# Block-sparse attention and a SoLU layer in one kernel: centring tile u in place of w_out, with a new operation order

## The chip, the core and the metric

The kernel runs on one core of a Trainium2 chip. The metric is the device time of one execution in microseconds (us); lower is better. The core has five engines with queues of their own: TensorE (PE in the profile; PEld is its weight load), VectorE (DVE), ScalarE (ACT), GpSimd (POOL) and SyncE (SP), which here issues nearly all DMAs.

## The reference

q, k and v have shape (4, 8, 768, 64): four batches, eight heads, 768 positions in 24 blocks of 32. The attention is masked by blocks; its output is put through a feed-forward layer with a softmax gate and a layer norm.

```python
scores = scale * np.matmul(q, k.transpose(0, 1, 3, 2))
mask = np.abs(blk_i - blk_j) <= 1
mask = mask | (blk_i == 0) | (blk_j == 0) | (blk_i == n_blocks - 1) | (blk_j == n_blocks - 1)
...  # three sampled blocks for each row of blocks are added to the mask
attn = softmax(np.where(mask, scores, -1e9));  x = attn @ v      # x: 3072 x 512
h = x @ w_in                                                     # 3072 x 1024
solu = h * softmax(h)
ln = (solu - mean(solu)) / np.sqrt(var(solu) + 1e-06) * g_ln
out = ln @ w_out                                                 # 3072 x 512
```

## The kernel before, in words

All matmuls are in bf16. The mask is part of the score: keys and queries have 64 columns of data and 24 more (KR = 88), a selector of the own block on the key's side and a row of penalties on the query's side, so that a forbidden pair gets a large negative score.

**Attention.** For each batch `b`, each third of the queries `t` (256 positions) and each pair of heads `pr`, `attend` issues three groups of four score matmuls into `sbank` (L561), three exponentials of 128 x 1024 on ACT (L568), one group of 24 matmuls with v (`pv`, L581) into an `mbank`, a reciprocal (L590) and a normalization into tile `x` (L593). That is 144 score groups, 144 exponentials and 48 pv groups.

**Feed-forward.** For each third, x is transposed by a DMA (L623) or, in the first and last third, by PE (L613). `feed` then treats two tiles of 128 positions. For a tile: two groups of four matmuls of 512 columns into `hbank` (L643), an exponential with its sum (silu_e, L666), the product u (L669), its statistics (L676, L679), then on POOL `z2` (L682), `vr` (L685) and the power -1/2 `rs` (L718). Tile u is transposed by a DMA from SP's queue (`cross_u`, L749; the first tile by PE, L741), two groups of four matmuls (`out4`, L759) multiply it by `w_out_sb`, the result is scaled by `rs` (L767 on ACT, L769 on DVE) and stored (L773). The last two tiles have parts of their own, in halves (L643 into `tbank`, L692, L696, L702, L729, L782). There are 24 tiles. A tile u is held until its transpose has been read; there are three.

**Centring of w_out.** The mean that the layer norm takes off is taken off the weights instead. `wg` (L439) scales each of the eight 128-row chunks of w_out by g into scratch, `cs` (L448) sums them over all rows with eight matmuls by a matrix of ones, `wb` (L451) divides by 1024, and `wo` (L453) scales each chunk again and subtracts that mean row. All `out4` need `wo`.

**Opening.** For batch 0, keys and queries are cast (L295, L293), transposed by PE (L477) and copied to `kT[0]` and `qT[0]`. The selector is made on POOL (L307, L310), transposed by PE (`selp_tp`, L324) and copied by ACT (`selp`). The penalty rows come from small DVE operations up to `bar_b` (L346), and from `mask2` (L350) and `mcol` (L359) on PE. For later batches, `crossed` casts a pair of heads (cast6), transposes it by a DMA (L533) and splits it into the two heads' rows (`split`); these copies run by list on DVE, POOL or ACT, all at line L295 or L293. w_in is staged in `kT[1]` and `qT[1]`, and the mask rows of these two are copied from `kT[0]` and `qT[0]` by two DMAs (`m1dma`, L811 and L812).

**Order.** The kernel makes a list of 1159 operations and emits them in an order that is written out by hand (`ORDER`); `ENGINES` says which of them run on another engine than the one in the code, and `SPARES` lists dummy matmuls (L823) that are put in the order. Each engine takes its operations in that order and waits at the head of its queue, SP included: a DMA that has to wait holds up all DMAs behind it.

Of the kernel before, what the change touches and what calls it, by code (L numbers as in the profile page):

```python
# [871 lines left out]
```

## Time and profile before

| | us |
|---|---|
| median of three runs (208.11 to 209.76) | 208.84 |
| the profiled execution | 210.25 |
| its span in the trace | 208.5 |
| PE busy / ACT busy / DVE busy / POOL busy | 200.3 / 179.4 / 138.8 / 84.2 |
| DMA moved | 43.19 MB, 207 GB/s mean |

A row of the groups reads: line, engine, operation, output<-input, shapes, count | busy us, mean ns of one | idle time of the engine just before them, and what ended it. A row of the timeline or of the chain reads: start us, length us, what. A row of one tile's view reads: line, engine, operation, count: duration ns min/median/max, first and last start. "SPq" is SP's queue.

### The profile page before, as it was taken

The page shows a single profiled execution, that of the slowest core. Times are in us where ns is not written, and L with a number is a line of the kernel's source. Part 1 is how long each engine was busy: PE and PEld are TensorE (multiplying, and loading weights), DVE is VectorE, ACT ScalarE, POOL GpSimd, SP SyncE. Part 2 cuts the span into 40 slices and gives each one's busy share as a digit, 9 for nine tenths or more (in the row PEclk, how much of TensorE's full clock was granted, in tenths as well). Part 3 has the DMA queues.
Part 4 walks back from the last instruction along what each step waited for, and adds up shares of the span by engine and source line. Part 5 has one row for each costly group of instructions (what it writes and reads, how often), then busy time and mean ns, then how long its engine had stood idle before and what let it go on. Part 6 is the DMA issues. An engine that isn't in the chain of part 4 may idle for free.

```text
span 208.5 us, 5748 instructions
## 1 busy us (share of the span) xinstructions
PE 200.3 (96%) x2282; PEld 142.0 (68%) x2313; DVE 138.8 (67%) x306; ACT 179.4 (86%) x230; POOL 84.2 (40%) x158
## 2 busy tenths in 40 slices
PE   8999999999999999999799999999999999999993
PEld 4798876756667768566566767666767758666452
DVE  5586689999887555757676864754755565485840
ACT  3599999998999999999599998989989898876683
POOL 4235398185540647316640731683320211001271
PEclk9999999999999999999999999999999999999999
DMA  5999995999999998999899989995393314672534
GB/s 142 336 358 347 384 361 123 205 226 287 211 222 327 311 189 208 254 263 286 230 299 228 233 185 251 207 257 126 101 127 99 63 19 104 151 105 53 122 134 152
DMA packets 71736, 43.19 MB, mean 207 GB/s; under 512 B 53348, under 2 KB 67180, under 8 KB 71660
## 3 DMA queue, kind: packets, MB, share of 16 engines
q1 hardware_dynamic: 71672, 42.81, 84.9%
q8 instruction: 18, 0.29, 0.6%
q14 instruction: 10, 0.08, 0.1%
q10 hardware_dynamic: 36, 0.00, 0.0%
HBM read 23.07 MB, written 6.29 MB: 141 GB/s over the span
## 4 chain that ended last, share of the span: by engine, by line
PE 73%; DVE 12%; DMA 7%; ACT 3%; issue 2%; SPq 1%; ACTq 0%
PE sbank L561 22%; PE mbank L759 15%; PE hbank L643 14%; PE mbank L581 13%; DMA qx<-qb 4%; DVE w_out_sb L453 3%; PE abank L477 3%; ACT ex L568 2%; DMA xT<-x 2%; DVE u L669 2%; PE tbank L643 2%; PE sbank L823 2%; DVE x L593 1%; DMA out_dram<-ot 1%; DVE w_in_sb L295 1%
## 5 line engine op out<-in xcount | busy, mean ns | idle before, releaser
L568 ACT ACTIVATE ex<-sbank 128x1024 bf16<-128x1024 f32 x144 | 141.0, 1025 | 15.7 <-PE sbank L561 14.2
L561 PE MATMUL sbank<-qT,kT 88*128 88x256 bf16 x576 | 81.5, 272 | 0.5 <-DVE qT L295 0.3
L561 PEld LDWEIGHTS <-kT 88*128 88x128 bf16 x576 | 52.7, 97 | 19.2 <-issue 0.9
L759 PE MATMUL mbank<-w_out_sb,uT 128*128 128x512 bf16 x175 | 45.0, 379 | 0.8 <-DVE w_out_sb L453 0.3
L581 PEld LDWEIGHTS <-ex 128*128 128x128 bf16 x1152 | 40.8, 97 | 7.0 <-issue 1.3
L581 PE MATMUL mbank<-va,ex 128*128 128x65 bf16 x1152 | 42.3, 193 | 1.4 <-DVE x L593 1.3
L643 PE MATMUL hbank<-w_in_sb,xT 128*128 128x512 bf16 x157 | 41.9, 378 | 1.4 <-DMA xT<-x 0.3
L669 DVE TENSOR_TENSOR u<-hbank,e 128x1024 bf16<-128x1024 f32 x22 | 26.8, 1216 | 19.6 <-ACT e L666 15.7
L676 DVE BATCH_NORM_STATS2 bs<-u 128x6 f32<-128x512 bf16 x44 | 29.2, 679 | 0.2
L643 PEld LDWEIGHTS <-xT 128*128 128x128 bf16 x192 | 18.2, 97 | 15.0 <-DMA xT<-x 0.8
L759 PEld LDWEIGHTS <-uT 128*128 128x128 bf16 x184 | 17.6, 97 | 14.6 <-issue 0.8
L590 DVE RECIPROCAL r<-mbank 128x4 f32<-128x4 f32 x48 | 8.3, 175 | 25.7 <-PE mbank L581 25.5
L666 ACT ACTIVATE e<-hbank 128x1024 bf16<-128x1024 f32 x22 | 22.5, 1024 | 1.3 <-PE hbank L643 1.3
L685 POOL TENSOR_SCALAR vr<-z,mv 128x1 f32<-128x1 f32 x22 | 5.8, 266 | 39.0 <-DVE mv L679 38.0
L593 DVE TENSOR_TENSOR x<-mbank,r 128x256 bf16<-128x256 f32 x48 | 19.7, 415 | 0.8
L718 POOL TENSOR_TENSOR rs<-vr,neg_half 128x1 f32<-128x1 f32 x24 | 13.8, 579 | 0.8
L295 POOL COPY qT<-kc 64x768 bf16<-64x768 bf16 x10 | 8.9, 889 | 11.7 <-DMA kc<-qb 6.1
L769 DVE TENSOR_SCALAR ot<-mbank,rs 128x512 f32<-128x512 f32 x13 | 9.7, 745 | 5.7 <-PE mbank L759 3.1
L682 POOL TENSOR_TENSOR z<-z 128x1 f32<-128x1 f32 x22 | 4.7, 212 | 20.1 <-ACT e L666 19.7
L295 POOL CAST kb<-kst 128x768 bf16<-128x768 f32 x7 | 6.2, 892 | 15.3 <-DMA kst<-in_k_dram 8.8
L295 POOL COPY kT<-kc 64x768 bf16<-64x768 bf16 x13 | 11.0, 844 | 2.6 <-DMA kc<-kb 2.2
L295 POOL CAST va<-vst 128x768 bf16<-128x768 f32 x8 | 6.6, 827 | 7.4 <-DMA vst<-in_v_dram 7.3
(110 smaller groups left out, 165.5 us busy)
## 6 DMA issues: line engine op xcount, KB each, us to landing
vst<-in_v_dram SPq DMA_DIRECT2D x16, 384.0 KB, 5.0
out_dram<-ot SPq DMA_DIRECT2D x23, 256.0 KB, 2.4
kst<-in_k_dram SPq DMA_DIRECT2D x15, 384.0 KB, 4.7
qst<-in_q_dram SPq DMA_DIRECT2D x12, 384.0 KB, 5.3
w_out_f<-in_moe_w_out_dram SPq DMA_DIRECT2D x2, 1024.0 KB, 8.4
qst<-in_q_dram SPq DMA_DIRECT2D x4, 256.0 KB, 5.9
...
```

The source lines that it names most:

```text
L295: (nc.vector if o.eng == "DVE" else nc.gpsimd).tensor_copy(out=dst, in_=src)
L561: nc.tensor.matmul(s[:, m, :], kT[i][0:KR, pr, jc, hh, :], qT[i][0:KR, pr, 2 * t : 2 * t + 2, hh, :], start=(m % 2 == 0), stop=(m % 2 == 1))
L568: exs.append(op("exp", "ACT", lambda o, so=so: nc.scalar.activation(out=exb[o.slot], in_=sbank[so.slot], func=ACT.Exp, scale=scale), [so], ...
L581: nc.tensor.matmul(acc(o)[:, qt, hh, :], exb[exs[n].slot][:, m, qt * P : (qt + 1) * P], va[i][:, 2 * pr + hh, jc, :], start=first, stop=(n ...
L593: nrm = op("norm", "DVE", lambda o: nc.vector.tensor_tensor(out=xb[x_of[b, t].slot][:, :, 2 * pr * D : (2 * pr + 2) * D].rearrange("p a (h ...
L643: nc.tensor.matmul(d, xTb[xt[0].slot][:, qt, c, :], w_in_sb[n][:, c, :], start=(c == 0), stop=(c == KD - 1))
L666: zs = op("silu_e", "ACT", lambda o: nc.scalar.activation(out=eb[o.slots["e"]], in_=hb(), func=ACT.Exp, accum_out=zb[o.slots["z"]][:, 0:1] ...
L669: us = op("mult", "DVE", lambda o: nc.vector.tensor_mul(out=ub[o.slot], in0=hb(), in1=eb[zs.slots["e"]]), [zs], take="u", last_of=[(hs[0], ...
L676: bs.append(op("stats", "DVE", lambda o, n=n: nc.vector.bn_stats(out=bsb[(bs[0] if bs else o).slot][:, n, :], in_=ub[us.slot][:, w(o, n)]) ...
L718: rs = op("rs", "POOL", lambda o: nc.gpsimd.tensor_tensor(out=rsb[o.slot], in0=vrb[vr.slot], in1=neg_half, op=ALU.pow), [vr, c2], take="rs ...
L759: nc.tensor.matmul(mbank[m0.slot], uTb[ut[0].slot][:, KF // 2 * n + f, :], w_out_sb[n][:, f, :], start=(n == 0 and f == 0), stop=(n == 1 a ...
L769: nc.vector.tensor_scalar(out=otb[o.slot], in0=mbank[os_[0].slot], scalar1=rsb[rs.slot], scalar2=None, op0=ALU.mult)
```

## The change

- **Centring.** `wg` scales each chunk of w_out once, straight into `w_out_sb`, and for 22 of the 24 tiles that is the weight. For these tiles the product becomes `multa`, with an accumulator that gives the mean, and a new pass `cent` takes the mean off u in place (ten on DVE, twelve on POOL), ahead of the transpose and of the statistics. The last two tiles keep uncentred u and take centred weights, made late: three sums over the chunks (`ws4`, `ws2`, `ws1`, on POOL), one matmul `cs`, and the eight `wo` on DVE, into the space of `kT[0]` and `qT[0]` once batch 2 has been read.
- **Selector.** `selp_tp` and the ACT copy go; four selects on POOL (two for the first two columns of blocks, two for the other four) make the transposed selector directly. `mask2` needs only the first part.
- **Mask rows.** The two mask DMAs (`m1dmb`) read only the first pair's rows and broadcast them, and each waits for four of the eight w_in casts. The splits of batch 1 wait for those w_in casts whose staging space they overwrite.
- **Order.** ORDER, ENGINES and SPARES are new (1187 operations; 36 dummy matmuls, most of them of 128 columns). 12 `z2` and 9 `vr` are on DVE, all eight `wo` on DVE, five of eight `wg` and four of eight w_in casts on POOL, five of 23 scales on ACT (ten before), of the k, q and v casts 11 on DVE (18 before). Two query loads are issued ahead of the first key load.

```diff
-    st = op("selp_tp", "PE", selp_tp, [own, mids], take="m")
-    sels = op("selp", "ACT", lambda o: copy(
-        o, selp.rearrange("a c p -> a (c p)"), mbank[st.slot].bitcast(BF16)[0:NB, 0 : NCH * P]), [st], last_of=[st])
+    sels = []
+    for c0, c1 in ((0, 2), (2, NCH)):
+        a = op(f"selp{c1 - c0}", "POOL", lambda o, c0=c0, c1=c1: nc.gpsimd.affine_select(
+            out=selp[:, c0:c1], in_=nc.const_aps.tensor(1.0, (NB, c1 - c0, P), BF16), compare_op=ALU.is_ge,
+            fill=0.0, base=c0, channel_multiplier=-BLK, pattern=[[1, c1 - c0], [NCH, P]]))
+        sels.append(op(f"selp{c1 - c0}", "POOL", lambda o, c0=c0, c1=c1: nc.gpsimd.affine_select(
...
-    def w_out_g(c):
-        return exb[wg[c - c % 2].slot].rearrange("p (a m) t -> p a (m t)", a=2)[:, c % 2, :]
     def weigh(o, c):
-        d, s, k = w_out_g(c), w_out_f[c // 4][:, c % 4, :], g_sb[:, c : c + 1]
+        d, s, k = w_out_sb[c // 4][:, c % 4, :], w_out_f[c // 4][:, c % 4, :], g_sb[:, c : c + 1]
...
-        for c in range(KF):
-            nc.tensor.matmul(mbank[o.slot], onesf, w_out_g(c), start=(c == 0), stop=(c == KF - 1))
...
+    def centred_weights(free):
...
+        s4 = op("ws4", e, lambda o: add(o, level[1], w_out_sb[0].rearrange("p c d -> p (c d)"),
+                                        w_out_sb[1].rearrange("p c d -> p (c d)")), wg + free)
+        s2 = op("ws2", e, lambda o: add(o, level[2], level[1][:, 0 : 2 * d], level[1][:, 2 * d :]), [s4])
+        tot = level[1].bitcast(BF16)[:, 0:d]
+        s1 = op("ws1", e, lambda o: add(o, tot, level[2][:, 0:d], level[2][:, d:]), [s2])
+        cs = op("cs", "PE", lambda o: nc.tensor.matmul(mbank[o.slot], onesf, tot, start=True, stop=True), [s1, c1],
+                take="m")
...
-            us = op("mult", "DVE", lambda o: nc.vector.tensor_mul(
-                out=ub[o.slot], in0=hb(), in1=eb[zs.slots["e"]]), [zs],
+            um = op("multa", "DVE", lambda o: nc.vector.scalar_tensor_tensor(
+                out=ub[o.slot], in0=hb(), scalar=1.0 / d_ff, in1=eb[zs.slots["e"]], op0=ALU.mult, op1=ALU.mult,
+                accum_out=zb[zs.slots["z"]][:, 1:2]), [zs],
                 take="u", last_of=[(hs[0], hp), (zs, ("e",))])
+            us = op("cent", "DVE", lambda o: (nc.vector if o.eng == "DVE" else nc.gpsimd).tensor_scalar(
+                out=ub[um.slot], in0=ub[um.slot], scalar1=float(d_ff), scalar2=zb[zs.slots["z"]][:, 1:2],
+                op0=ALU.mult, op1=ALU.subtract), [um], last_of=[um, (zs, ("z",))])
...
-            mask1["k"] = op("m1dma", "SP", lambda o: nc.sync.dma_start(out=kT[1][MC], in_=kT[0][MC]), kdone + w_in_b)
-            mask1["q"] = op("m1dma", "SP", lambda o: nc.sync.dma_start(out=qT[1][MC], in_=qT[0][MC]), qdone + mq0 + w_in_b)
+            for nm, a, dep in (("k", kT, kdone[:2]), ("q", qT, [ready_q[0, 1, 0][0]] + mq0)):
+                mask1[nm] = op("m1dmb", "SP", lambda o, a=a: nc.sync.dma_start(
+                    out=a[1][MC], in_=a[0][MC, 0:1].broadcast_to([NB, NPR, NCH, 2, P])),
+                    dep + [w_in_n[n][c + (0 if nm == "k" else 2)] for c in range(2) for n in range(2)])
```

More of the change, by code (lines that the diff above doesn't have):

```diff
@@ L319 @@
     kheld = [own1] + kown[1:]
-    def selp_tp(o):
-        d = mbank[o.slot].bitcast(BF16)
-        for c in range(NCH):
-            nc.tensor.matmul(d[0:NB, c * P : (c + 1) * P], kc[0][:, c, 0, MC], ident, is_transpose=True,
-                             start=(c == 0), stop=(c == NCH - 1))
-    st = op("selp_tp", "PE", selp_tp, [own, mids], take="m")
-    sels = op("selp", "ACT", lambda o: copy(
-        o, selp.rearrange("a c p -> a (c p)"), mbank[st.slot].bitcast(BF16)[0:NB, 0 : NCH * P]), [st], last_of=[st])
+    sels = []
[4 more added lines that the diff above has]
+        sels.append(op(f"selp{c1 - c0}", "POOL", lambda o, c0=c0, c1=c1: nc.gpsimd.affine_select(
+            out=selp[:, c0:c1], in_=selp[:, c0:c1], compare_op=ALU.is_ge, fill=0.0, base=BLK - 1 - c0,
+            channel_multiplier=BLK, pattern=[[-1, c1 - c0], [-NCH, P]]), [a]))
     d2 = op("small", "DVE", lambda o: nc.vector.tensor_tensor(out=dist, in0=iota_d, in1=iota_d, op=ALU.mult),
@@ L340 @@
     static = op("small", "DVE", lambda o: nc.vector.memset(bar[1][:, 0 : NB : NB - 1], 0.0), [b1])
-    iof = op("small", "DVE", lambda o: nc.vector.tensor_copy(out=iota_f, in_=iota_k), [ik])
-    slo = op("small", "DVE", lambda o: nc.vector.tensor_copy(out=samp_f, in_=samp_i[:, :, 0]), [samp_dma])
+    iof = op("conv", "DVE", lambda o: copy(o, iota_f, iota_k), [ik])
+    slo = op("conv", "DVE", lambda o: copy(o, samp_f, samp_i[:, :, 0]), [samp_dma])
     prev, dep = bar[1], [static, iof, slo]
@@ L417, with staged @@
         for n in range(2)]
-    w_in_b = w_in_n[0] + w_in_n[1]
+    def staged(nm, pr):
+        c0 = 0 if nm == "k" else 2
+        return [w_in_n[n][c0 + c] for c in ((0,), (0, 1), (1,), ())[pr] for n in range(2)]
     g_load = op("g", "SP", lambda o: nc.sync.dma_start(out=g8, in_=moe_g_ln.rearrange("(c p) -> c p", p=P)))
@@ L440, in weigh @@
                                                                        op0=ALU.mult)
-    for c in range(KF):
-        wg.append(op("wg", "DVE", lambda o, c=c: weigh(o, c), [w_out_load[c // 4], g_cp],
-                     take=None if c % 2 else "ex", after=wg[c - 1 :] if c % 2 else ()))
-    def cs_mm(o):
-        for c in range(KF):
-            nc.tensor.matmul(mbank[o.slot], onesf, w_out_g(c), start=(c == 0), stop=(c == KF - 1))
-    cs = op("cs", "PE", cs_mm, wg + [c1], take="m", last_of=wg[::2])
@@ L451 @@
-    wb = op("wbar", "ACT", lambda o: nc.scalar.mul(out=wbar, in_=mbank[cs.slot], mul=1.0 / d_ff), [cs],
-            last_of=[cs])
-    wo = [op("wo", "DVE", lambda o, c=c: (nc.vector if o.eng == "DVE" else nc.gpsimd).scalar_tensor_tensor(
-        out=w_out_sb[c // 4][:, c % 4, :], in0=w_out_f[c // 4][:, c % 4, :], scalar=g_sb[:, c : c + 1],
-        in1=wbar, op0=ALU.mult, op1=ALU.subtract), [wb]) for c in range(KF)]
+    wg = [op("wg", "DVE", lambda o, c=c: weigh(o, c), [w_out_load[c // 4], g_cp]) for c in range(KF)]
@@ new lines, with add @@
+    w_end = kT[0].rearrange("p a b c d -> p (a b c d)")[:, 0 : KF * d_model].rearrange("p (f d) -> p f d", f=KF)
+    w_sum = qT[0].rearrange("p a b c d -> p (a b c d)").bitcast(FP32)
+    def centred_weights(free):
+        e, d = "DVE", d_model
+        level = [None, w_sum[:, 0 : 4 * d], w_sum[:, 4 * d : 6 * d]]
+        def add(o, dst, a, b):
+            (nc.vector if o.eng == "DVE" else nc.gpsimd).tensor_tensor(out=dst, in0=a, in1=b, op=ALU.add)
+        s4 = op("ws4", e, lambda o: add(o, level[1], w_out_sb[0].rearrange("p c d -> p (c d)"),
[5 more added lines that the diff above has]
+                take="m")
+        wb = op("wbar", "ACT", lambda o: nc.scalar.mul(out=wbar, in_=mbank[cs.slot], mul=1.0 / d_ff), [cs],
+                last_of=[cs])
+        return [op("wo", "DVE", lambda o, c=c: nc.vector.scalar_tensor_tensor(
+            out=w_end[:, c, :], in0=w_out_f[c // 4][:, c % 4, :], scalar=g_sb[:, c : c + 1], in1=wbar,
+            op0=ALU.mult, op1=ALU.subtract), [wb]) for c in range(KF)]
@@ L458 @@
+    w_last = []
     last_use = {}
@@ L465, in cast_v @@
         i = b % 2
-        ready_v[(b, pr)] = op("cast6", "POOL", lambda o: copy(
+        ready_v[(b, pr)] = op("cast6" if b == 0 else "castb", "POOL", lambda o: copy(
             o, va[i][:, 2 * pr : 2 * pr + 2, :, 0:D], vst[ld.slot]),
@@ L470, with turned @@
     a_ops = []
-    def turned(pr, src, held, s0, c0, c1, dst, deps, eng, release=(), rows=KR):
+    def turned(pr, src, held, s0, c0, c1, dst, deps, eng, release=(), rows=KR, after=()):
         n = c1 - c0
@@ L478, in tp @@
                                  ident, is_transpose=True, start=(k == 0), stop=(k == 2 * n - 1))
-        t = op(f"turn{2 * n}", "PE", tp, deps + [mids], take="a", last_of=release)
+        t = op(f"turn{2 * n}", "PE", tp, deps + [mids], take="a", last_of=release, after=after)
         a_ops.append(op(f"evac{2 * n}", eng, lambda o: copy(
@@ L499, in opening @@
             gq = turned(pr, qa, cq, 0, 0, 2, qT[0], [cq], "DVE", [cq], rows=D)
-            ga = turned(pr, kc, ck, 0, 0, 2, kT[0], [ck] + kown, "ACT", [ck])
+            ga = turned(pr, kc, ck, 0, 0, 2, kT[0], [ck, kown[0]], "ACT", [ck], after=kown)
             gb = turned(pr, kc, ck, 2, 2, 6, kT[0], [cr], "DVE", [ck] + kheld)
@@ L508, in opening @@
             gq = turned(pr, qa, cq, 0, 0, 2, qT[0], [cq] + qown, "DVE", [cq])
-            ga = turned(pr, kc, ck, 0, 0, 4, kT[0], [ck] + kown, "DVE", [ck] + kheld)
+            ga = turned(pr, kc, ck, 0, 0, 4, kT[0], [ck, kown[pr % NKC]], "DVE", [ck] + kheld, after=kown)
             gb = turned(pr, kc, ck, 4, 4, 6, kT[0], [ck], "DVE", [ck] + kheld)
@@ L530, in crossed @@
         st, cb, cx, dst = (kst, kb, kx, kT) if nm == "k" else (qst, qb, qx, qT)
-        ca = op("cast6", "POOL", lambda o: copy(
+        ca = op("castb", "POOL", lambda o: copy(
             o, cb[o.slot], st[ld.slot].rearrange("p h c d -> p c h d")), [ld], take=nm + "b", last_of=[ld])
@@ L536, in crossed @@
         for hh in range(2):
-            got.append(op("split", "DVE", lambda o, hh=hh: copy(
+            got.append(op("split", "POOL", lambda o, hh=hh: copy(
                 o, dst[i][0:D, pr, :, hh, :], cx[t.slot][hh * D : hh * D + D]),
-                [t, last_use.get((b - 2, pr))] + (w_in_b if b == 1 else []), last_of=[t]))
-        got += ([mask1["k"]] if nm == "k" else [mask1["q"]]) if b == 1 else []
+                [t, last_use.get((b - 2, pr))] + (staged(nm, pr) if b == 1 else []), last_of=[t]))
+        got += [mask1[nm]] if b == 1 else []
         if nm == "k":
@@ L676, in feed @@
                 bs.append(op("stats", "DVE", lambda o, n=n: nc.vector.bn_stats(
[L677 to L678 removed]
+                    out=bsb[(bs[0] if bs else o).slot][:, n, :], in_=ub[um.slot][:, w(o, n)]),
+                    [us] + bs, take=None if n else "bs", last_of=[um]))
             mv = op("aggr", "DVE", lambda o: nc.vector.bn_aggr(
@@ L748, in feed, with w2 @@
         else:
-            ut = [op("cross_u", "SP", lambda o: nc.sync.dma_start_transpose(out=uTb[o.slot], in_=ub[u0.slot]), [u0],
+            ut = [op("cross_u", "SP", lambda o: nc.sync.dma_start_transpose(out=uTb[o.slot], in_=ub[u0.slot]), [us],
                      take="uT", last_of=[u0])] * 2
         HD = d_model // 2
+        if last and not w_last:
+            w_last.extend(centred_weights([last_use[B - 2, pr] for pr in range(NPR)]))
+        wn = w_last if last else wg
+        def w2(f):
+            return w_end[:, f, :] if last else w_out_sb[f // 4][:, f % 4, :]
         if j < NF - 1:
@@ L782, in outp @@
                         nc.tensor.matmul(mbank[o.slot][:, 0:HD], uTb[ut[0].slot][:, f, :],
-                                         w_out_sb[f // 4][:, f % 4, cols], start=(f == 0), stop=(f == KF - 1))
-                oo = op("outh", "PE", outp, ut + wo, take="m", last_of=[ut[0]])
+                                         w2(f)[:, cols], start=(f == 0), stop=(f == KF - 1))
+                oo = op("outh", "PE", outp, ut + wn, take="m", last_of=[ut[0]])
                 def scaled(o, cols=cols, oo=oo):
```

38 lines of the change are left out of this document (19 added, 19 removed), and 118 rows, old and new, of tables (ENGINES, ORDER, SPARES).

## The prediction

> **What bounds the kernel now.** I read the page first (busy time, chain that ended last), then the chain in order of time, then busy time by stage, then the tiles that the change touches.
>
> ```profile
> PE 200.3 (96%) x2282; PEld 142.0 (68%) x2313; DVE 138.8 (67%) x306; ACT 179.4 (86%) x230; POOL 84.2 (40%) x158
> PE 73%; DVE 12%; DMA 7%; ACT 3%; issue 2%; SPq 1%; ACTq 0%
> ```
>
> A busy PE need not be a full one, so I count its work. The chain in order of time has the price of each group of matmuls when nothing is in its way (start, length, what); the group rows of the weight loads have the counts.
>
> ```profile
> 8.20 0.44 PE sbank L561 x4
> ...
> 12.30 0.45 PE abank L477 x8
> ...
> 20.55 0.73 PE mbank L581 x24
> ...
> 55.19 0.86 PE mbank L759 x4
> ...
> 64.52 0.86 PE hbank L643 x4
> ...
> 203.49 1.87 PE mbank L782 x16
> ```
> ```profile
> L561 PEld LDWEIGHTS <-kT 88*128 88x128 bf16 x576 | 52.7, 97 | 19.2 <-issue 0.9 <-DVE qT L295 0.4 <-POOL kT L295 0.4
> L581 PEld LDWEIGHTS <-ex 128*128 128x128 bf16 x1152 | 40.8, 97 | 7.0 <-issue 1.3 <-DVE x L593 0.5 <-ACT ex L568 0.4
> L643 PEld LDWEIGHTS <-xT 128*128 128x128 bf16 x192 | 18.2, 97 | 15.0 <-DMA xT<-x 0.8 <-issue 0.6
> L759 PEld LDWEIGHTS <-uT 128*128 128x128 bf16 x184 | 17.6, 97 | 14.6 <-issue 0.8
> ```
>
> Scores 144 x 0.44 = 63.4 us, pv 48 x 0.73 = 35.0, feeds 48 x 0.86 = 41.3, outputs 46 x 0.86 + 1.87 = 41.4; the transposes (8 in 0.45) come to about 8, the column sum of w_out to 8 matmuls of 0.215 = 1.7. That is 190.6 of useful PE work in a span of 208.5. The first score is at 8.2 and the last matmul ends at 205.4; about 0.9 of the work lies ahead of 8.2, so only some 7.5 us in between are lost. Busy time by stage shows where:
>
> ```profile
> 30.00:50.00 20.00, 19.23 (x202) 13.16 (x205) 19.87 (x35) 18.82 (x26) 12.55 (x16) 1.00 0.94 213
> 50.00:100.00 50.00, 49.55 (x570) 35.01 (x577) 34.47 (x72) 46.94 (x56) 23.01 (x40) 1.00 1.12 247
> 100.00:110.00 10.00, 8.47 (x96) 5.89 (x94) 6.80 (x15) 7.68 (x10) 4.78 (x9) 1.00 1.14 284
> 110.00:190.00 80.00, 78.77 (x927) 55.70 (x940) 49.42 (x108) 71.24 (x88) 23.42 (x48) 1.00 0.71 148
> ```
>
> Columns: stage, length, then PE, PEld, DVE, ACT, POOL busy with instruction counts, clock, DMA. From 50 to 100 and from 110 on PE is full at clock 1.00: nothing on another engine is worth time there, and any new wait costs its full length. Gains can come from PE work left out, from the start, from 30 to 50 (DVE busy 19.87 of 20) and from 100 to 110.
>
> **The change, part by part.** *w_out.* Before, w_out is scaled into scratch (L439), summed over its rows by 8 matmuls (L448) and scaled again with the mean taken off (L453).
>
> ```profile
> 34.34 1.89 PE L448 MATMUL mbank<-ex,onesf 128*128 128x512 bf16 x7
> ```
> ```profile
> L453 DVE SCALAR_TENSOR_TENSOR w_out_sb<-w_out_f,g_sb,wbar x8: 733/743/2075, 37.1 to 47.1; 128x512 bf16<-128x512 f32 x8
> L439 POOL TENSOR_SCALAR ex<-w_out_f,g_sb x4: 1812/1899/2243, 24.7 to 31.1; 128x512 bf16<-128x512 f32 x4
> L439 DVE TENSOR_SCALAR ex<-w_out_f,g_sb x4: 475/762/1034, 26.1 to 33.1; 128x512 bf16<-128x512 f32 x4
> ```
>
> Now one matmul of 0.215 is left: 7 x 0.215 = **-1.5 us** of PE work, and it is full value since PE is what is short. The eight L453 passes (7.9 us in all) leave the stage in which DVE is full. One L439 pass goes from DVE to POOL. DVE there gets three centring passes instead, 1 to 3 us. PE lost 0.8 us of idle time in this stage and about as much again in slow groups; ACT, 18.8 of 20 busy, allows 1.2: I take **-1.0** (0 to -1.5). The eight L453 passes come back late, for the last two tiles: three sums on POOL (3584 columns; 4 to 14 us between POOL's copy and L439 rows below), listed about 50 us of PE work ahead of the last two tiles' outputs, then 8 x 0.74 = 5.9 us on DVE spread over the last 40 us. DVE had 49.42 of 80 there, so most of it is covered; without that cover the tail waits for it. **+0.3** (0 to +1.5).
>
> *Tile u.* The product (L669) gets an accumulator, and a second pass takes off the mean in place; ten of these on DVE, twelve on POOL.
>
> ```profile
> L669 DVE TENSOR_TENSOR u<-hbank,e x2: 1224/1224/1225, 66.7 to 72.9; 128x1024 bf16<-128x1024 f32 x2
> DMA to landing us min/median/max: 3.2/3.8/5.6
> ```
> ```profile
> L666 ACT ACTIVATE e<-hbank 128x1024 bf16<-128x1024 f32 x22 | 22.5, 1024 | 1.3 <-PE hbank L643 1.3
> L666 ACT ACTIVATION_READ_ACCUMULATOR e<-hbank 128x1 f32 x22 | 4.6, 207 | 0.0
> L676 DVE BATCH_NORM_STATS2 bs<-u 128x6 f32<-128x512 bf16 x44 | 29.2, 679 | 0.2
> L696 DVE DVE_READ_ACCUMULATOR u<-tbank,e 128x1 f32 x4 | 0.3, 82 | 0.0
> ```
> ```profile
> DMA to landing us min/median/max: 3.1/3.2/3.2
> ```
>
> The accumulator adds 0.08: 22 x 0.08 = 1.8 us of DVE, hidden under PE. On DVE a centring pass lies between the 64x768 copies of this engine (0.34 for 768 columns at their shortest, so 0.45 for 1024; a row is quoted under the rivals, with its delay) and the statistics row L676 (0.68 for 512, so 1.4); I take 0.6, as both ends are 16-bit tiles in SBUF like the copy's. The path that matters is silu, product, centring, transposing DMA, out4: 1.23 + 1.30 + centring + 3.8 us (3.1 after 140 us). Between a tile's second feed and its first out4, the new order lists this PE work at its tightest POOL tiles: first tile of batch 1, 7 scores, 2 pv, 4 feed or output groups = 8.0 us; third pair of batch 0, first tile, 8.9; first tile of batch 2, 8.7; third tile of batch 2, 9.2; third tile of batch 3, 8.3. Before, the tightest were 8.0, 8.4 and 8.4, with 6.3 needed. So a centring pass is free up to 1.7 us; from there PE waits. What does POOL need for 1024 columns?
>
> ```profile
> L295 POOL COPY kT<-kc 64x768 bf16<-64x768 bf16 x13 | 11.0, 844 | 2.6 <-DMA kc<-kb 2.2
> L439 POOL TENSOR_SCALAR ex<-w_out_f,g_sb 128x512 bf16<-128x512 f32 x4 | 7.8, 1963 | 3.1 <-PE mbank L581 3.1
> ```
>
> From below, the copy: 844 x 4/3 = 1.1 us. From above, the nearest operation, L439 on POOL: 1.96 for 512 columns, so 3.9 by columns; by bytes (3 KB in and out there at 1.81, its fastest; 4 KB here) 2.4. I take 2.4, since the operation is L439's but the input half as wide: need 8.73, so only the first of these tiles waits, **+0.7** (0 to +7.2). The Trainium skill (GPSIMD Engine Reference, Engine selection) holds one-input elementwise work on GpSimd to run near line rate; by it a pass would be about 1.1 and this term 0. L439, a one-tensor pass at 1.96 us for 512 columns, does not agree, so the row decides.
>
> *Selector.* The PE transposes and the ACT copy of it go; four selects on POOL over 24 partitions come.
>
> ```profile
> L324 PE MATMUL mbank<-ident,kc 128*24 128x128 bf16 x6 | 0.8, 309 | 0.0
> L293 ACT COPY selp<-mbank 24x768 bf16<-24x768 bf16 x1 | 0.8, 789 | 0.8 <-PE mbank L324 0.8
> L307 POOL TENSOR_SCALAR_AFFINE_SELECT kc<-const-bfloat16-1.0 128x144 bf16<-128x144 bf16 x1 | 0.4, 353 | 0.4 <-POOLq L856 0.4
> ```
>
> By the 144-column row, 256 and 512 columns take 0.5 and 0.8 at one column per ns after a fixed 0.2: 2.6 us of POOL, ahead of the cast of the first keys. The mask matmul then waits for neither PE nor ACT; but key loads are now issued behind two query loads. First score 0.8 earlier to 0.5 later: **-0.4**.
>
> *Mask copy and w_in.* The mask DMAs waited at the head of SP's queue, with later loads behind them:
>
> ```profile
> SPq L812 <- DVE w_in_sb L295: 8.1, 1, 8.1
> ```
> ```profile
> L295 POOL CAST w_in_sb<-qT 128x512 bf16<-128x512 f32 x1 | 0.6, 610 | 2.6 <-DMA qT<-in_moe_w_in_dram 2.6
> L685 POOL TENSOR_SCALAR vr<-z,mv 128x1 f32<-128x1 f32 x22 | 5.8, 266 | 39.0 <-DVE mv L679 38.0
> ```
>
> Now each waits for four w_in casts, four of the eight casts run early on POOL (4 x 0.61, hidden under ACT's exponentials), and w_in is loaded sooner, so feeds can fill PE earlier between 8 and 30 us: **-0.5** (0 to -1.5). Casts, splits, scales and 21 one-column operations of the variance (0.27 each by L685, so up to 5.7 us that go to DVE) change engine; PE, full, covers them, and without that cover DVE has 15 us free from 50 to 100 and 30 from 110 to 190.
>
> *Order.* From 100 to 110 PE lost 1.5 us:
>
> ```profile
> 93.21 7.35 DMA qx<-qb
> 100.59 0.56 DVE qb L295
> ```
>
> A DVE cast waited for a transposing DMA, and behind it in DVE's queue stood the norm that pv needed. Casts that wait so are fewer on DVE (8 in the new list, with 17 splits); the wait can vanish or come elsewhere: -1.5 to +1.5, taken as **-0.4**.
>
> Sum: -1.5 - 1.0 + 0.3 + 0.7 - 0.4 - 0.5 - 0.4 = **-2.8 us**. The profiled execution took 210.25 (span 208.5, 1.75 around it) and would take 207.4; it ran 1.4 above the median of the three runs, 208.84, so the forecast is 206.0.
>
> **Rivals.** (a) *Centring on POOL costs what L439 does by the column, 3.9 us; slower.* Need 10.2 (9.5 late); the five tiles lack 2.2, 1.3, 1.5, 1.0 and 1.2, together 7.2, in place of 0.7: 206.0 + 6.5 = 212.5. It decides from the price at which the five lacks reach 3.5, about 3.1 us; past 3.5 us it is over 1% slower. For: same operation, same engine. Against: a 16-bit input, and copies at 0.84. The Trainium skill (GPSIMD Engine Reference, Key points) warns that GpSimd shares its SBUF interfaces with VectorE; the trace shows that too: beside a POOL copy one DVE copy took 1.03 that takes 0.34 alone.
>
> ```profile
> 49.95 0.82 POOL L295 COPY kT<-kc 64x768 bf16<-64x768 bf16 x1
> 49.96 1.03 DVE L295 COPY kT<-kc 64x768 bf16<-64x768 bf16 x1
> ...
> 91.01 0.34 DVE L295 COPY kT<-kc 64x768 bf16<-64x768 bf16 x1
> ```
>
> (b) *The early stage has a second bound.* ACT at 18.82 of 20 keeps the pace from 8 to 50 us, the two early terms (-1.5) bring nothing: 207.5. For: ACT's exponentials run back to back there. Against: PE is short in the end, and less work is less work.
>
> (c) *The new order has stalls of its own.* Two waits of the 100-to-110 kind in place of one: -0.4 becomes +1.5, and with the full 1.5 in the tail 209.1. For: 25 DVE casts and splits that wait for DMAs. Against: PE's idle time outside that stage is small.
>
> **How the numbers follow.** A measurement here tells about 1% from no change, 206.8 and 210.9. Forecast 0.48 (faster 0.44, within 1% 0.04; its own range 203.4 to 207.2, the low end being 1.5 of PE work, the start and half of the 7.5 lost). (a) 0.25: slower 0.18, within 1% 0.07. (b) 0.18: faster 0.03, within 1% 0.15. (c) 0.09: within 1% 0.05, slower 0.04. So faster 0.47, same 0.31, slower 0.22. The range reaches up into (a) as far as a POOL pass of 3.7 us (+2.8): 203.4 to 211.6.
>
> **What would show it.** Right: one column-sum matmul; DVE not full from 30 to 50; first score near 7.8; PE full outside the start; centring rows on POOL under 2.5 us and no PE idle time ahead of out4 but in the first tile of batch 1. Wrong: centring on POOL above 3.1 us with PE waiting for uT; PE idle from 100 to 110 as before, or elsewhere for a DMA; the last two tiles waiting for the second weights.

## The result, and the profile after

The changed kernel takes 232.24 us (median; 230.01 to 234.8), the kernel before, run beside it, 209.3 (208.11 to 210.31): a ratio of 1.107 [1.100, 1.115], some 22 us slower. Ratios leave disturbed executions out, so they need not be the quotient of the medians. The profiled execution took 230.01, its span is 228.3.

The first lines of the page of the changed kernel: busy time, and the chain that ended last by engine.

```profile
PE 202.2 (89%) x2271; PEld 141.2 (62%) x2301; DVE 149.7 (66%) x353; ACT 179.7 (79%) x227; POOL 141.6 (62%) x164
POOL 33%; PE 26%; DVE 13%; DMA 13%; issue 9%; ACT 2%; SPq 2%; POOLq 0%; DVEq 0%; ACTq 0%
```

POOL, off the chain before, is a third of it; PE falls from 73 to 26%. By stage (columns as before: PE, PEld, DVE, ACT, POOL, clock, DMA):

```profile
30.00:50.00 20.00, 19.09 (x218) 13.22 (x219) 16.83 (x39) 19.55 (x25) 16.34 (x17) 1.00 1.15 241
50.00:100.00 50.00, 44.34 (x470) 29.58 (x475) 28.39 (x67) 39.60 (x49) 37.32 (x35) 0.97 1.01 223
100.00:110.00 10.00, 7.57 (x111) 5.59 (x110) 8.08 (x20) 7.38 (x9) 7.37 (x7) 1.00 0.73 138
110.00:190.00 80.00, 72.84 (x817) 50.76 (x827) 51.89 (x112) 66.10 (x78) 46.30 (x48) 0.98 0.67 151
```

PE lost 0.5 us from 50 to 100 before and loses 5.7 now; from 110 to 190, 1.2 before and 7.2 now. From 30 to 50 DVE is no longer full (16.83 for 19.87), yet PE did not gain. The groups of the centring, and the page's row of the statistics behind it:

```profile
L685 POOL TENSOR_SCALAR u<-u,z 128x1024 bf16<-128x1024 bf16 x12 | 44.8, 3732 | 19.6 <-DVE u L680 15.7
L691 DVE BATCH_NORM_STATS2 bs<-u 128x6 f32<-128x512 bf16 x44 | 29.4, 683 | 27.7 <-POOL u L685 27.5
...
L685 DVE TENSOR_SCALAR u<-u,z 128x1024 bf16<-128x1024 bf16 x10 | 5.6, 563 | 0.1
```

A pass on POOL costs 3.73 us, on DVE 0.56. And DVE stood 27.5 us for POOL, at the head of its queue with the statistics. The timelines of DVE and then of POOL show one such wait (in brackets: idle time before, and what ended it):

```profile
88.47 0.15 DVE L697 TENSOR_TENSOR z<-z 128x1 f32<-128x1 f32 x1
91.21 1.29 DVE L691 BATCH_NORM_STATS2 bs<-u 128x6 f32<-128x512 bf16 x2 [2.59 <-POOL u L685]
92.41 1.21 DVE L680 SCALAR_TENSOR_TENSOR u<-hbank,e 128x1024 bf16<-128x1024 f32 x1
93.55 0.08 DVE L680 DVE_READ_ACCUMULATOR u<-hbank,e 128x1 f32 x1
93.74 0.75 DVE L798 TENSOR_SCALAR ot<-mbank,rs 128x512 f32<-128x512 f32 x1
94.41 0.34 DVE L297 COPY qT<-kc 64x768 bf16<-64x768 bf16 x1
```
```profile
87.45 3.73 POOL L685 TENSOR_SCALAR u<-u,z 128x1024 bf16<-128x1024 bf16 x1 [0.51 <-DVE u L680]
```

Behind the waiting statistics stand the next tile's product, the scaling that frees an `mbank`, and a split: work that PE needs and that has nothing to do with this tile's mean. The waits of PE itself (total us, times, longest):

```profile
PEld L788 <- DMA uT<-u: 4.9, 3, 2.0
PE mbank L788 <- DMA uT<-u: 4.3, 3, 1.9
PE mbank L592 <- DVE x L604: 3.9, 3, 2.0
PEld L572 <- DVE qT L297: 2.5, 2, 2.2
PE sbank L572 <- POOL qT L297: 2.4, 2, 2.2
```

Only part is the forecast's wait, uT ahead of out4 (L788); pv and scores wait for what DVE and POOL do later. What follows a pause can be slow as well. PE's timeline:

```profile
54.77 1.57 PE L788 MATMUL mbank<-w_out_sb,uT 128*128 128x512 bf16 x4 [1.92 <-DMA uT<-u]
56.13 1.06 PE L572 MATMUL sbank<-qT,kT 88*128 88x256 bf16 x4
56.98 1.80 PE L788 MATMUL mbank<-w_out_sb,uT 128*128 128x512 bf16 x4
58.62 0.60 PE L572 MATMUL sbank<-qT,kT 88*128 88x256 bf16 x4
```

The scores take 1.06 behind the pause and 0.60 some 2.5 us later, and the granted clock from 50 to 60 is 0.83, where it was 1.00 before. Over the whole span it is 0.985 (1.00 before), some 3.4 us' worth.

### The profile page after: what moved, and what is told of

The parts are those of the page before. It is cut to its first block, busy times and chain, and to the rows that moved or that the text cites. A ratio compares the mean times of both kernels' runs of the same rounds, so it can differ in the third digit from the quotient of the medians.

```text
span 228.3 us, 5768 instructions
## 1 busy us (share of the span) xinstructions
PE 202.2 (89%) x2271; PEld 141.2 (62%) x2301; DVE 149.7 (66%) x353; ACT 179.7 (79%) x227; POOL 141.6 (62%) x164
## 4 chain that ended last, share of the span: by engine, by line
POOL 33%; PE 26%; DVE 13%; DMA 13%; issue 9%; ACT 2%; SPq 2%; POOLq 0%; DVEq 0%; ACTq 0%
POOL u L685 17%; PE sbank L572 8%; PE mbank L788 7%; PE mbank L592 5%; DMA vst<-in_v_dram 5%; PE hbank L654 4%; DMA qT<-in_moe_w_in_dram 4%; DVE u L680 4%; POOL w_out_sb L440 4%; DMA qx<-qb 2%; DVE bs L691 2%; POOL rs L740 2%; POOL qT L297 2%; ACT e L677 2%; SPq L378 2%
## 5 line engine op out<-in xcount | busy, mean ns | idle before, releaser
L579 ACT ACTIVATE ex<-sbank 128x1024 bf16<-128x1024 f32 x144 | 140.5, 1024 | 29.3 <-PE sbank L572 28.0
L572 PE MATMUL sbank<-qT,kT 88*128 88x256 bf16 x576 | 84.4, 274 | 5.6 <-POOL qT L297 2.4
L572 PEld LDWEIGHTS <-kT 88*128 88x128 bf16 x576 | 53.2, 98 | 28.6 <-issue 7.4
L685 POOL TENSOR_SCALAR u<-u,z 128x1024 bf16<-128x1024 bf16 x12 | 44.8, 3732 | 19.6 <-DVE u L680 15.7
L788 PE MATMUL mbank<-w_out_sb,uT 128*128 128x512 bf16 x163 | 45.1, 394 | 6.6 <-DMA uT<-u 4.3
L691 DVE BATCH_NORM_STATS2 bs<-u 128x6 f32<-128x512 bf16 x44 | 29.4, 683 | 27.7 <-POOL u L685 27.5
L654 PE MATMUL hbank<-w_in_sb,xT 128*128 128x512 bf16 x160 | 42.9, 379 | 1.0
L680 DVE SCALAR_TENSOR_TENSOR u<-hbank,e 128x1024 bf16<-128x1024 f32 x22 | 26.7, 1213 | 8.0 <-ACT e L677 7.9
L788 PEld LDWEIGHTS <-uT 128*128 128x128 bf16 x184 | 17.9, 100 | 20.9 <-DMA uT<-u 4.9
L740 POOL TENSOR_TENSOR rs<-vr,neg_half 128x1 f32<-128x1 f32 x24 | 14.7, 614 | 12.4 <-DVE vr L703 11.3
L604 DVE TENSOR_TENSOR x<-mbank,r 128x256 bf16<-128x256 f32 x48 | 19.7, 416 | 0.8
L798 DVE TENSOR_SCALAR ot<-mbank,rs 128x512 f32<-128x512 f32 x18 | 13.4, 742 | 4.0 <-POOL rs L740 2.6
L706 POOL TENSOR_SCALAR vr<-z,mv 128x1 f32<-128x1 f32 x13 | 3.6, 278 | 15.4 <-DVE mv L694 14.8
L297 POOL COPY qT<-kc 64x768 bf16<-64x768 bf16 x8 | 6.6, 829 | 8.3 <-DMA kc<-qb 8.0
L297 POOL CAST va<-vst 128x768 bf16<-128x768 f32 x9 | 7.4, 825 | 6.2 <-DMA vst<-in_v_dram 6.1
L297 POOL CAST qb<-qst 128x768 bf16<-128x768 f32 x10 | 8.6, 858 | 0.2
```

What stands on the lines that cost most here:

```text
L297: (nc.vector if o.eng == "DVE" else nc.gpsimd).tensor_copy(out=dst, in_=src)
L572: nc.tensor.matmul(s[:, m, :], kT[i][0:KR, pr, jc, hh, :], qT[i][0:KR, pr, 2 * t : 2 * t + 2, hh, :], start=(m % 2 == 0), stop=(m % 2 == 1))
L579: exs.append(op("exp", "ACT", lambda o, so=so: nc.scalar.activation(out=exb[o.slot], in_=sbank[so.slot], func=ACT.Exp, scale=scale), [so], ...
L604: nrm = op("norm", "DVE", lambda o: nc.vector.tensor_tensor(out=xb[x_of[b, t].slot][:, :, 2 * pr * D : (2 * pr + 2) * D].rearrange("p a (h ...
L654: nc.tensor.matmul(d, xTb[xt[0].slot][:, qt, c, :], w_in_sb[n][:, c, :], start=(c == 0), stop=(c == KD - 1))
L680: um = op("multa", "DVE", lambda o: nc.vector.scalar_tensor_tensor(out=ub[o.slot], in0=hb(), scalar=1.0 / d_ff, in1=eb[zs.slots["e"]], op0 ...
```

## The experiments

Each is set against the kernel before, run on the same chip beside it; a point below is one per cent of its time, 2.1 us.

**1. All centring on DVE.** The twelve `cent` leave POOL's list; the order stays.

```diff
-        11, 22, 108, 110, 113, 114, 115, 339, 356, 533, 549, 566, 615, 776, 792, 809, 1019, 1035, 1052, 1108, 1109,
-        1110,
+    "POOL": [11, 22, 108, 110, 113, 114, 115, 1108, 1109, 1110],
```

> The changed kernel with all 22 centring passes on DVE (the twelve POOL passes of 3.73 us become DVE passes of about 0.56), same order. Theory 1 (PE and DVE wait for the POOL pass): nearly all of the loss goes, 205 to 210 us, and the 27.5 us that the statistics on DVE wait for POOL's u are gone. Theory 2 (the new order, its start and its DMA waits are worse by themselves): still above 220. Theory 3 (POOL is too busy for the casts and splits of keys and queries): as theory 1 here, since POOL falls from 142 to about 97 us.

Ratio 1.0144 [1.0083, 1.0204]. Of 10.7 points 9.3 (19 us) come from the twelve passes on POOL. The other 1.4 are looked for in experiment 7.

**2. The same passes on POOL, for nobody.** They read `w_in_sb`, write a scratch tile, and nothing waits for them; twelve tiles stay uncentred.

```diff
-                out=ub[um.slot], in0=ub[um.slot], ...
+                out=sqb[0], in0=w_in_sb[0][:, 0:2, :].rearrange("p c d -> p (c d)"), ...
...
+            us = um
```

> The changed kernel with the twelve POOL passes at their places and of their length, but reading other data and writing to a scratch tile, and nothing waits for them (those tiles stay uncentred and scaled by 1/1024). POOL is as busy as before, about 140 us. Theory 1 (waits for u): 205 to 211. Theory 3 (POOL's queue is late with casts, splits and rs): most of the loss stays, 222 or more. A part of each would lie between.

Ratio 1.0398 [1.0329, 1.0468]: POOL's time by itself, which puts its splits, casts, `z2` and `rs` off, is 2.5 points. The other 6.7 (14 us) are waits for the centred u and, for a smaller part, the cast of experiment 6, which is not held here. Could the passes instead hold DVE's own copies, as POOL's copy did in the forecast's row? Rows of POOL and DVE in this kernel speak against it; this cast takes its usual time in the midst of a pass:

```profile
59.15 3.71 POOL L686 TENSOR_SCALAR sq<-w_in_sb,z 128x1024 bf16<-128x1024 bf16 x1 [0.97 <-DVE u L680]
61.34 0.53 DVE L297 CAST kb<-kst 128x768 bf16<-128x768 f32 x1
```

**3. The statistics later.** The twelve tiles' `stats`, `aggr`, `vr` and `rs` are listed 6 us of PE work behind their `cent`; the pass stays as it is.

```diff
-ORDER: ... cent (POOL), stats, stats, aggr, [other DVE work], ...
+ORDER: ... cent (POOL), [other DVE work], stats, stats, aggr, ...
```

> The changed kernel with the twelve POOL passes as they are, but the statistics, their aggregation, the variance and rs of those twelve tiles moved back in the order until 6 us of PE work lie behind the pass's place, so that DVE does not stand waiting with reciprocals and normalizations queued behind. Theory 1 with the wait in DVE's queue as the main part: 10 to 15 us of the 23 come back, 217 to 222, and the DVE wait for POOL's u falls from 27.5 us to under 5. Theory 1 with the path to out4 as the main part (the lack that the prediction's rival a added up to 7): at most 5 come back, 227 or more. Theories 2 and 3: no change, 230 to 233.

Ratio 1.0711 [1.0637, 1.0785], 3.6 points better. In the waits of this kernel

```profile
DVE bs L687 <- POOL u L681: 2.6, 1, 2.6
PEld L784 <- DMA uT<-u: 8.1, 5, 2.3
PE mbank L784 <- DMA uT<-u: 6.8, 4, 2.0
```

DVE's wait has gone from 27.5 to 2.6 us, and PE's wait for uT has grown from 4.3 to 6.8: a part of the 6.7 points went through DVE's queue, the rest remains on the way from the pass to out4. The 3.6 points are not the queue's alone, since in this order the cast of experiment 6 is not held either (0.55 us); that experiment sets the shares.

**4. A short pass.** POOL centres 128 of 1024 columns (the other columns stay uncentred).

```diff
+                e, n = (nc.vector, d_ff) if o.eng == "DVE" else (nc.gpsimd, 128)
+                e.tensor_scalar(out=ub[um.slot][:, 0:n], in0=ub[um.slot][:, 0:n], ...
```

> The changed kernel with the twelve POOL passes over the first 128 of the 1024 columns only (the rest of those tiles is left uncentred and unscaled): the same places, queues and dependencies, but a pass of about 0.6 us in place of 3.73. Theory 1 (it is the pass's length): 205 to 210. Theory 2: above 220. If a chain through POOL's queue is itself the cost, whatever the length: between, 213 to 220.

Ratio 1.0280 [1.0195, 1.0366], with 0.76 us a pass. Even then it is 1.4 points above DVE. POOL comes to the pass late in its own queue, but that this is the reason is not shown: here the cast of experiment 6 is held too (3.69 us, and PE waits 2.1 for it), which may be all of the difference.

**5. What the pass costs, and a cheaper form.** Four forms of the twelve passes, three tiles each, which differ in what they compute, in one run:

```diff
+ nc.gpsimd.tensor_scalar(u, u, d_ff, 0.5, mult, subtract)      # two operations, constants
+ nc.gpsimd.tensor_scalar(u, u, mean, subtract)                 # one operation
+ nc.gpsimd.tensor_scalar(u, u, d_ff, mult)                     # one operation, constant
+ nc.gpsimd.tensor_tensor(u, u, mean.broadcast, subtract)       # two tensors
```

> The changed kernel with the twelve POOL passes in four other forms, three tiles each, so that the price of each form can be read in the trace: (0) two operations with constants only, (1) one operation, subtraction of the per-partition mean, (2) one operation, multiplication by a constant, (3) a two-input subtraction with the mean broadcast along the row (each leaves out a part of the centring or of the scaling). If the per-partition scalar makes the pass dear, forms 0 and 2 take about 1.1 us like a copy and form 1 about 3.7. If the second operation does, forms 1 and 2 take about half of form 0. If it is the instruction as such, 0, 1 and 2 all take about 3.7 us (3.6 ns a column, the rate of the w_out scaling); a two-input form by the sums of w_out (2048 columns in 4.05 us, 512 in 1.27) takes about 2.2.

The groups, in that order of lines:

```profile
L691 POOL TENSOR_SCALAR u<-u 128x1024 bf16<-128x1024 bf16 x3 | 11.0, 3663 | 5.1 <-DVE u L681 5.1
L694 POOL TENSOR_SCALAR u<-u,z 128x1024 bf16<-128x1024 bf16 x3 | 8.6, 2854 | 8.6 <-DVE u L681 4.9 <-DVE r L602 3.7
L696 POOL TENSOR_SCALAR u<-u 128x1024 bf16<-128x1024 bf16 x3 | 8.4, 2793 | 3.7 <-DVE u L681 3.7
L698 POOL TENSOR_TENSOR u<-u,z 128x1024 bf16<-128x1024 bf16 x3 | 5.9, 1975 | 4.3 <-DVE u L681 4.3
```

The per-partition operand costs nothing (2.85 to 2.79), a second operation 0.9, and the form with two tensors is the cheapest. So the changed kernel, whole, with that form:

```diff
-                out=ub[um.slot], in0=ub[um.slot], scalar1=float(d_ff), scalar2=zb[zs.slots["z"]][:, 1:2],
-                op0=ALU.mult, op1=ALU.subtract), [um], last_of=[um, (zs, ("z",))])
+                    nc.gpsimd.tensor_scalar(out=m, in0=m, scalar1=1.0 / d_ff, scalar2=None, op0=ALU.mult)
+                    nc.gpsimd.tensor_tensor(out=u, in0=u, in1=m.broadcast_to([P, d_ff]), op=ALU.subtract)
```

> The changed kernel with the twelve centrings still on POOL, but in the form that took 1.89 us by itself: a subtraction of two tensors, the mean broadcast along the row, after one 128x1 multiplication that makes the mean of the sum (some 0.4 us). What the forecast's sum stands on (a pass of 2.4 us or less costs 0.7 us in all) would give 206 to 208, ratio 0.985 to 1.00. Theory A (POOL is the wrong place because the statistics at the head of VectorE's queue, and uT, wait for POOL's turn, whatever the pass costs above the length that fits): between the short pass, 1.028, and the full one, 1.107; by the length of the pass (2.3 of 3.7 us, and 0.5 us for the short one) 1.06 to 1.08. Rival B (only what POOL's time is over about 2.5 us counts): 1.02 to 1.035, as with the short pass.

Ratio 1.0405 [1.0333, 1.0478], between the two expectations (1.06 to 1.08 by length, 1.02 to 1.035): 1.55 us less a pass (1.91 and 0.27 for 3.73) brings 6.7 points, 14 us or 1.2 us a tile. Two rows of it:

```profile
L694 POOL TENSOR_TENSOR u<-u,z 128x1024 bf16<-128x1024 bf16 x12 | 22.9, 1908 | 1.0
...
L693 POOL TENSOR_SCALAR z<-z 128x1 f32<-128x1 f32 x12 | 3.3, 273 | 21.2 <-DVE u L682 17.5 <-DVE r L602 3.7
```

DVE still waits 10.7 us for u here. The same with the statistics later, as in experiment 3:

> The two-tensor form on POOL, and the statistics, the variance and the power of the twelve tiles listed 6 us of TensorE's work behind the centring (the order of the run with the statistics later). Theory A (the rest is VectorE's queue): the wait of the statistics for POOL's u, 10.7 us, goes, and the time falls by 2 to 4 us, ratio 1.020 to 1.03. Rival B (the rest is what POOL's 26 us more of work put late: splits, casts, z2 and rs): ratio stays 1.035 to 1.045.

Ratio 1.0421 [1.0316, 1.0526]: no gain, though the wait is no longer among DVE's. Two things have changed here, however: the cast of experiment 6, held for 3.87 us in the kernel above, takes 0.88 in this order, which by itself is worth 1.9 points below. So listing the statistics later costs elsewhere about what it saves: PE's waits for uT grow from 1.9 to 3.1 us, and a wait of 3.3 for the scaling that frees an `mbank` comes up. What the queue's head is worth at this price stays open.

**6. One cast of v beside a POOL sum.** In the changed kernel one cast of seven on DVE is long, while POOL makes the first column sum for the late weights (timelines of DVE and POOL):

```profile
161.51 0.41 DVE L604 TENSOR_TENSOR x<-mbank,r 128x256 bf16<-128x256 f32 x1
161.84 3.88 DVE L297 CAST va<-vst 128x768 bf16<-128x768 f32 x1
165.64 1.21 DVE L680 SCALAR_TENSOR_TENSOR u<-hbank,e 128x1024 bf16<-128x1024 f32 x1
```
```profile
161.25 4.05 POOL L452 TENSOR_TENSOR qT<-w_out_sb,w_out_sb 128x2048 f32<-128x2048 bf16 x1
```

The cast ends 0.4 us after the sum, and pv waits for it: PE is busy 7.49 of 10 us there. That one cast goes to ACT, in the changed kernel and in the one with the cheap form:

```diff
     "ACT": [
-        ... 652, 877, 890, ...
+        ... 652, 877, 878, 890, ...
     "DVE": [
-        ... 873, 876, 878, 885, ...
+        ... 873, 876, 885, ...
```

> The changed kernel, with the one cast of v that met POOL's sum on ScalarE in place of VectorE; all else as it is. Theory A (POOL's two-tensor sum holds VectorE's cast to its end and the wait for pv behind it is felt in full): the 3.9 us cast is gone, TensorE's clock stays at 1.00 between 160 and 170 us, and the time is 2 to 4 us below that of the changed kernel, ratio 1.09 to 1.10. Rival B (the stage is late anyway for POOL's u; another operation of VectorE is held instead): ratio stays near 1.107.

> The same in the kernel with POOL's pass in the two-tensor form (1.0405). Theory A: TensorE is full between 150 and 160 us in place of 7.24 of 10, and 2 to 3 us go, ratio 1.025 to 1.032. Rival B: 1.036 to 1.045.

Ratios 1.0940 [1.0815, 1.1064] for 1.1072, where the intervals overlap, and 1.0220 [1.0122, 1.0319] for 1.0405, where they just do not: 1.9 points, 3.9 us, for one cast, with 1.2 points either way. In the first, the stage 160 to 170:

```profile
160.00:170.00 10.00, 9.59 (x71) 6.25 (x71) 5.85 (x16) 6.30 (x8) 8.29 (x11) 0.83 0.35 80
```

PE is busy 9.59 for 7.49; the clock, expected at 1.00, stays at 0.83. With the cheap form and this cast moved, centring on POOL is 0.8 points above centring on DVE (no such cast is held in either kernel), inside what two such ratios can tell apart.

The kernel with 1.0940 is the one to read experiments 2 and 3 against, since the cast is held in none of the three. From it, not waiting for u brings 5.4 points, and the later statistics 2.3 of these: some two fifths of the waits went through DVE's queue. As far as such shares add, the 10.7 points are 1.4 for the order, 2.5 for POOL's time, 1.3 for the cast, 2.3 for DVE's queue and 3.1 for the rest of the way to out4; the cast and the queue are uncertain by about 1.4 each, the rest (from 1.0711 to 1.0398, neither with a held cast) by 1.0.

**7. The early stage.** First the forecast's own term: the kernel before with one of its eight column-sum matmuls (the mean row is then that of one chunk).

```diff
-        for c in range(KF):
-            nc.tensor.matmul(mbank[o.slot], onesf, w_out_g(c), start=(c == 0), stop=(c == KF - 1))
+        nc.tensor.matmul(mbank[o.slot], onesf, w_out_g(KF - 1), start=True, stop=True)
```

> The kernel before with one of the eight column-sum matmuls (the weights' mean is then wrong), which is the one term of the prediction that was PE work left out: 7 x 0.215 = 1.5 us. If PE is the bound in that stage as the prediction had it: ratio 0.993, 1.5 us less. If the stage from 30 to 50 us has DVE as its bound: no difference, ratio 0.998 to 1.002.

Ratio 1.0021 [0.9975, 1.0067]: nothing. Its stage from 30 to 50:

```profile
30.00:50.00 20.00, 18.31 (x209) 12.78 (x210) 19.90 (x35) 19.22 (x26) 11.09 (x11) 1.00 0.85 172
```

PE is busy 18.31 where it was 19.23: what was saved became idle time, since DVE sets the pace. The chain of the kernel before, which the forecast read in order of time, lies on DVE from 28.6 to 48.4, but for short stretches of issue; some of its pieces:

```profile
32.06 2.09 DVE ex L439 x3
...
38.37 1.98 DVE w_out_sb L453 x3
...
40.95 1.95 DVE w_out_sb L453 x2
```

Then the 1.4 points of experiment 1. From 40 to 70, the kernel before and the one with all centring on DVE:

```profile
40.00:70.00 30.00, 29.27 (x337) 20.45 (x340) 26.40 (x50) 27.83 (x34) 15.01 (x23) 1.00 1.11 262
```
```profile
40.00:70.00 30.00, 24.40 (x244) 16.13 (x246) 20.51 (x50) 23.24 (x28) 16.12 (x23) 0.96 1.15 244
...
100.00:110.00 10.00, 9.89 (x133) 7.31 (x133) 9.08 (x23) 9.10 (x12) 4.29 (x9) 1.00 1.00 199
```

There 4.9 us of PE go; elsewhere it gains (from 100 to 110, 9.89 for 8.47). The chain of that kernel (start, length, what):

```profile
36.66 6.07 DMA xT<-x
...
48.14 6.74 DMA uT<-u
...
59.56 5.57 DMA kc<-kb
```

In the kernel before, the same DMAs issued from 25 to 65 us (count, median us to landing):

```profile
kc<-kb SPq DMA_TRANSPOSE x4, 3.7
uT<-u SPq DMA_TRANSPOSE x3, 4.8
...
xT<-x SPq DMA_TRANSPOSE x2, 4.7
```

So these three land 1.4 to 1.9 us later than the middle one of their kind. By kind, with all centring on DVE, kc takes 5.6 and xT 6.1 in the same window; of uT only this one is late, the next two take 4.6 and 4.4. Why? First, POOL's five scalings of w_out, suspected of making the crossings late, on DVE:

```diff
-    "POOL": [11, 22, 108, 110, 113, 114, 115, 1108, 1109, 1110],
+    "POOL": [11, 22, 1108, 1109, 1110],
```

> As e1 (all centring on DVE), and the five scalings of w_out that POOL has (8.3 us, between 29.8 and 40.6) are put on DVE, next to its own three, so that POOL casts keys and queries of batch 1 without a gap. Theory A (POOL's scalings delay the casts, the crossings of batch 1 bunch up and PE lacks kT and uT from 40 to 70 us): the stage's loss of about 7 us shrinks to 3 or less, 207 to 210 us, level with the kernel before or below. Theory B (the stage is short because of the order of loads and transposing DMAs): no change against e1, ratio to before still 1.01 or more.

Ratio 1.0189 [1.0101, 1.0277]; no gain, and SP issues the crossings when it did. Next SP's own list, the loads behind the crossings, out4 later, and both:

```diff
-SP: xT, mask rows, load k, load q, cross q, cross k, load k, load v, cross k, uT, cross q, load v, load q, uT, cross q, load v, load k, xT, cross k, uT
+SP: xT, mask rows, cross q, cross k, load k, load q, cross k, uT, load k, load v, cross q, uT, cross q, load v, load q, xT, cross k, load v, load k, uT
```

> All 22 tiles centred on VectorE, as in the run of that kind, and in SP's list eight loads of k, q and v between 38 and 60 us are put behind the crossings that they stood ahead of (two behind the crossings of k and q that left at 41 and 42 us, two behind the first uT, which left at 48.1, two behind the next, two behind the crossing of k that left at 59.6), with two casts of v and q set back to suit. Theory A (the remaining 1.4% is SP's queue: it is occupied without a gap from 36.7 to 64.5, and the loads hold the crossings up): the first uT leaves by 46, the waits of 2.0 us for uT near 53 and of 2.5 for kc near 64 shrink, and the time is 1.5 to 3 us below that of the kernel with all tiles on VectorE, ratio 1.000 to 1.007. Rival B (the crossings are late because of what feeds them, the casts on POOL; the loads go with them): same as before the move, 1.012 to 1.018, or slower, as the casts behind the later loads come late.

> All 22 tiles on VectorE; the two out4 groups of the first batch's second tile and the scaling behind them are listed 2 us of TensorE's work later. Theory A (TensorE stands for the first uT only because out4 is listed too early for it, and the work behind has its operands): the 2.0 us wait near 53 goes, and the time falls by 1 to 2 us, ratio 1.005 to 1.010. Rival B (the stage is short of operands as a whole; TensorE waits at the next instruction instead, for kc near 64): ratio stays 1.012 to 1.018.

> Both edits: the eight loads behind the crossings and the two out4 groups 2 us of work later. If both theories A hold, 0.995 to 1.004, level with the kernel before; if neither, 1.012 to 1.02.

Ratios 1.0119 [1.0056, 1.0183], 1.0137 [1.0078, 1.0196] and 1.0125 [1.0058, 1.0192]: none differs from 1.0144. With the loads behind, uT and the crossings of k land in 4 to 5 us and PE is full from 50 to 60, but the xT of 37.2 us lands after 7.8 and PE is busy 7.42 of 10 from 40 to 50. The gap moved. Last, the transfer of kT's mask rows, issued just behind that xT, put behind the next two crossings: alone, with the loads, and with out4 later as well.

```diff
-SP: xT, mask rows of kT, ..., cross q, cross k
+SP: xT, ..., cross q, cross k, mask rows of kT
```

> All tiles on VectorE; the transfer of kT's mask rows (288 KB) is issued two crossings later, behind the crossings of q and k that followed xT. Theory A (it shares the DMA engines with xT and makes it late): xT lands in 4.5 to 5 us instead of 6.1, the crossings behind it leave 0.8 us sooner, the time falls by 1 to 2 us, ratio 1.004 to 1.009. Rival B (transposing transfers that follow one another are slow by themselves): xT still 6 us or more, ratio 1.012 to 1.018.

> The same with the eight loads also behind the crossings. Theory A: the wait for xT near 43 to 45 us (2.2 us with the loads moved alone) goes, ratio 1.000 to 1.006. Rival B: 1.010 to 1.016.

> The same and the two out4 groups of the second tile 2 us of TensorE's work later. Theory A: 0.996 to 1.004, TensorE full between 40 and 70 us. Rival B: 1.010 to 1.016, with the gap at another place of that stretch.

Ratios 1.0123 [1.0071, 1.0175], 1.0190 [1.0124, 1.0256] and 1.0264 [1.0205, 1.0322]. xT lands in 5.7 us alone, little better than 6.1, and PE stands elsewhere; the timeline of the first of the three:

```profile
48.84 1.01 PE L565 MATMUL sbank<-qT,kT 88*128 88x256 bf16 x4 [3.87 <-POOL rs L733]
```

That the mask rows are what makes xT late is not borne out; whether the loads slow the crossings behind them (kc fell from 5.6 to 4.2 us without them) is not excluded. What holds is only that PE loses time in this stage in every order tried (busy 22.9 to 27.2 of 30 from 40 to 70, 29.27 before), mostly at a crossing or at the copy behind it; why the new order's crossings are later than the old one's is open.

## Why the prediction was wrong

It forecast 206.0 and a range of 203.4 to 211.6. The steps that failed, the dearest first:

- **"I take 2.4, since the operation is L439's but the input half as wide."** The pass takes 3.73. Of the two ways to carry L439 over to 1024 columns, by bytes and by columns, the second (3.9) was nearly right; the half as wide input made it little cheaper. At the price that was assumed the term would nearly have held: the cheap form costs 2.18 us a tile, and with the cast moved it is 0.8 points, some 1.6 us (give or take 2.4), above DVE, where the sum had 0.7. The Trainium skill (GPSIMD Engine Reference, Engine selection) holds one-input work to run near line rate. By the estimate from that a pass would take about 1.1; the trace contradicts it, since the one-tensor pass takes 2.8 even with one operation, and POOL's two-tensor form (1.91) is the quicker one.
- **"...a centring pass is free up to 1.7 us; from there PE waits."** Only the way over uT to out4 was counted. Rival (a), with 3.9 us, had the price, and it gave 7.2 us of lacks for what cost 19. That is about what its own way cost: its sum, worked out the same way at 3.73, is 6.5 us, and 3.1 points, 6.5 us, are left for it (experiment 6). Missing were the statistics at the head of DVE's in-order queue (2.3 points, experiments 3 and 6) and POOL's own later work (2.5, experiment 2). The sum named no work queued behind the new wait, though it added one on DVE for each of twelve tiles. The pauses then cost clock as well.
- **Late weights, "+0.3 (0 to +1.5)".** PE's longest waits name none of the eight DVE passes, so these were covered as forecast. The sums on POOL were not: one held a DVE cast to its end, which costs 3.9 us with the cheap form; in the changed kernel it is 2.8 us, of which the intervals do not exclude nothing. The row of a DVE copy held by a POOL copy was quoted, under rival (a), and not applied to a sum of 4 us.
- **"...it is full value since PE is what is short": -1.5 and -1.0.** The first was worth nothing (experiment 7), and of the second nothing came either (PE busy 19.09 from 30 to 50 as changed, 19.23 before). PE is short over the whole span, but from 30 to 50 DVE was; the row with 19.87 of 20 was quoted. Rival (b), a second bound there, was right, with DVE in ACT's place. Relieved of DVE (experiment 1's kernel), the stage has ACT busy 19.32 of 20 and meets its transposing DMAs from 40 to 70.
- **Order, -0.4; the stall from 100 to 110.** As changed, the stage is worse (7.57 busy, 8.47 before); with the centring on DVE it is gone (9.89). The order was better there, and POOL hid it.
- **Selector, -0.4.** Right: the first score comes at 7.63 for 8.20, and one column-sum matmul is left. **Mask copy and w_in, -0.5.** From 10 to 30 nothing was gained: PE is busy 19.58 of 20, 19.87 before.

```profile
7.63 0.61 PE L572 MATMUL sbank<-qT,kT 88*128 88x256 bf16 x4 [0.31 <-DVE kT L297]
```
